# The first block of an adaLN block with an S4 convolution and a SwiGLU FFN: rows of the running sum added by VectorE, statistics taken by ScalarE, weights split in one operation, and another order at the beginning

## The chip, the cores and the metric

The kernel runs on one core of a Trainium2 chip, in float32 results. The metric is device time in microseconds (us) of one execution. Before the change three executions took 484.87, 486.02 and 486.14 us, so the median is 486.02 us.

The engines are named as the profile names them: PE is TensorE (matmul) and PEld its weight load, DVE is VectorE, ACT is ScalarE, POOL is GpSimd, SP is SyncE, which issues most DMAs. Each engine runs its own instructions in the order in which they stand in its queue, and waits at the first one whose inputs are not there. A trailing "q" (ACTq) is the engine's sequencer, which issues DMAs.

## The reference

```python
def _layernorm(x, eps=1e-5): return (x - mean(x)) / sqrt(var(x) + eps)      # over the 448 channels

x = A_u                                                    # 2048 rows x 448 channels
sa, ca, ga, sb, cb, gb = (silu(c) @ w_mod) in six rows of 448
h = _layernorm(x) * (1 + ca) + sa
x = x + ga * (causal_conv(h, K) + h * Dskip)               # K[d, l] = Re sum_n C dB exp(dt A l), 256 states
h = _layernorm(x) * (1 + cb) + sb
x = x + gb * ((silu(h @ w_gate) * (h @ w_up)) @ w_down)    # 448 -> 1792 -> 448
```

The reference does the convolution with FFTs of length 4096. The kernel sums the 256 states into a constant and a linear part of K when a flag, computed on the chip from the data, says that this is exact enough (it is so for these inputs). The convolution is then a running sum down the rows: a triangular matrix of ones times the scaled rows, plus what was summed up to the tile before. A general path stands beside it, behind a branch on the flag, and is not run here.

## The kernel before, in words

The 2048 rows are 16 tiles of 128, in blocks of 2, 2, 3, 3, 3 and 3 tiles (`BLOCKS`). For each block a loop goes over f = 0 to 13, the 14 slices of 128 of the 1792 hidden units. In step f, `gate_up(f)` computes gate and up for the whole block: 22 matmuls (L729) of 128x128 weights against 256 or 384 columns. Weights and data are held as a high part, rounded to the fast matmul format, and a low part with the rest, so each product is high*high + low*high + high*low. A bank is a slice of PSUM. ACT then makes `p`, the silu of gate (L744), DVE multiplies it with up (L757), ACT rounds the product to `phi` (L760), and DVE takes the rest `plo` (L761). Then `down(f-1)` adds the product of the step before into the output accumulators (L773, three matmuls for each tile). So PE does gate_up(f) while the hidden units of f-1 are made ready.

Between the two, at half-steps given by the table `TIMES`, stands what the next block needs: number 2f is the place after `gate_up(f)` and ahead of `down(f-1)`, 2f+1 the place after `down(f-1)`. For the first block the steps of each following tile are `n1.stat` (mean and variance of the rows, two operations of DVE, L150 and L151), `n1.root` (1/sqrt, on POOL, L167 and L168), `s0` (the normalized rows, L182 and L184), `s1` (two products with the kernel's coefficients, L908), `s4f` (the running sum on PE, L945 to L948, then two DVE operations L927 and L950), `s5` (the result added to the tile, L960 and L961, and the last rows of the sum copied to `run` by ACT, L957, and DVE, L958, and sent to partition 0 by a DMA that ACT issues, L959), `n2.stat`, and at the end `n2.root` and `make_xn` (L193 on DVE, L194 and L195 on ACT). After gate_up(13) the tiles are turned (transposed) by PE (L206) into `hhi` and `hlo`, which the next block's gate_up reads.

`s4f` takes in the running sum of the tile before by two float32 matmuls with a single row: `pe.matmul(s, f32(tri[0:1, :]), run1[0:1], ...)` (L947) and the same for run0 (L948).

The first block also prepares the weights, which stay on the chip for the later blocks. In step f the weights of f+2 are split: `split_w` casts 1024 elements of each partition on ACT (L123), which are four chunks of channels for gate and four for up, the fourth of which has only 64 channels and holds them twice; DVE takes the rest of three chunks each (L125, 768 elements) and later that of the second copy in the fourth (L127, 256 elements on 64 partitions). `split_d` does the same for the down weight of f (L115 on ACT, `wdh`; L117 on DVE, `wdl`).

The beginning, up to the first matmul of gate_up(0), has its order written by hand: `PLAN` is a list of names of steps, and each engine issues its instructions in that order. In it the first two tiles are convolved, their statistics taken (L150, L151), normalized (`n10` and `n11`, L432, `xn0` and `xn1`, L487), turned by PE (`tr0`, `tr1`, L374 and L377), and cast to `hhi` (L423) and `hlo` (L428). A matmul (L472) with ones and a copy from PSUM spread the vector gb over the partitions. `first_rows` stands behind down's first place: ACT copies the last rows of the running sum (L696) and the first tile's rows (L697) out of PSUM, DVE adds (L698), and a DMA takes the row to partition 0 (L699).

Of the kernel before, what the change touches and what calls it, by code (L numbers as in the profile page):

```python
# [27 lines left out]
MB = max(BLOCKS)  # L28
# [15 lines left out]
m1 k1 cpc gd h11 hd0 ck v01 sq0 o10 v10 w0 cbw o12 v11 w01 o01 o02 hd1 o13 o14 xh1 gc0 sa st0 fs sp gq r0 n10 spc x1 xn0 gc1 st1 sbt tr0  # L44
qtb sbc r1 fl n11 l1 gbk hi00 xn1 w02 tr1 hi01 lo00 hi1 lo01 lo1 d00 d01 w1 w11 gb w12"""
# [11 lines left out]
def tile_kernel(ctx, tc, x, a_re, a_im, b_re, b_im, c_re, c_im, log_dt,  # L57
# [61 lines left out]
    def split_w(j, part=None, en=ve):  # L119
        hi, lo, st = wgu[j][:, :, 0:3, :], wgu[j][:, :, 4:7, :], wgu[j][:, :, 3, :]  # L120
        w = raw[j]
        if not part:
            sc.copy(wgu[j][:, :, 0:4, :], w)  # L123
        if part is None or part == 1:
            en.tensor_tensor(lo, w[:, :, 0:3, :], f32(hi), op=OP.subtract)  # L125
        if part is None or part == 2:
            en.tensor_tensor(st[64:128], w[64:128, :, 3, :], f32(st[64:128]), op=OP.subtract)  # L127
# [6 lines left out]
    run0, run1 = run[:, 0, :], run[:, 1, :]  # L134
    ca1 = const.tile([128, D], F32)
# [8 lines left out]
    flag = const.tile([1, 1], I32)  # L144

# [7 lines left out]
    class Norm:  # L153
# [10 lines left out]
        def root(self, ts):  # L164
            rs = small.tile([128, MB], F32, name="rs" + self.tag)
            n = len(ts)
            po.tensor_scalar(rs[:, 0:n], self.mv[:, 0:n, 1], EPS, None, op0=OP.add)  # L167
# [101 lines left out]
    with tc.tile_pool(name="pre", bufs=1) as pre:  # L269
# [23 lines left out]
        ve.memset(mhalf, -0.5)  # L293
        tiny = pre.tile([1, 1], F32)
# [74 lines left out]
        def turned_to(ps, t):  # L369

            for k in range(4):
# [38 lines left out]
        def to_channels(q):  # L410
            pk[q] = bank()
            turned_to(pk[q], h2[q])
# [7 lines left out]
        def high(q, ks=range(4)):  # L420
            for k in ks:
                c_ = slice(q * 128, (q + 1) * 128)
                sc.activation(hhi[:, k, c_], pk[q][:, k * 128:(k + 1) * 128], AF.Identity, bias=sbc[:, k:k + 1])  # L423

        def low(q, ks=range(4)):
            for k in ks:
                c_ = slice(q * 128, (q + 1) * 128)
                ve.scalar_tensor_tensor(hlo[:, k, c_], pk[q][:, k * 128:(k + 1) * 128], sbc[:, k:k + 1], f32(hhi[:, k, c_]),  # L428
                                        op0=OP.add, op1=OP.subtract)
# [7 lines left out]
        def flag_sum():  # L437
            pe.matmul(psm["d"][0:1, 460:462], ones, sz, start=True, stop=True)

        def flag_of():  # L440
            zm = pre.tile([1, 1], F32)
            ve.tensor_reduce(zm, psm["d"][0:1, 460:462], axis=AX.X, op=OP.add)
# [28 lines left out]
            "qtb": copy(gb, lambda: psm["gq"][:, 0:D]), "gb": copy(gb, lambda: psm["gq"][:, 0:D]),  # L471
# [15 lines left out]
            **{f"xn{q}": (lambda q: lambda: sc.activation(h2[q], h2[q], AF.Copy, scale=n2.of[q][1]))(q) for q in range(2)},  # L487
            **{f"tr{q}": do(to_channels, q) for q in range(2)}, "hi1": do(high, 1),
            **{f"hi0{z}": do(high, 0, (2 * z, 2 * z + 1)) for z in range(2)},
            "lo1": do(low, 1),  # L490
            **{f"lo0{z}": do(low, 0, (2 * z, 2 * z + 1)) for z in range(2)},

            "w0": do(split_w, 0, 0), "w01": do(split_w, 0, 1, WV), "w02": do(split_w, 0, 2, WV),
            "w1": do(split_w, 1, 0), "w11": do(split_w, 1, 1), "w12": do(split_w, 1, 2),
            **{f"d0{z}": do(split_d, 0, z) for z in range(2)},
# [197 lines left out]
    def first_rows():  # L693

        e = slice(96, 128)
        sc.copy(run1[e], CV[e, 0:D])  # L696
# [374 lines left out]
```

## Time and profile before

| what | value |
|---|---|
| three executions | 484.87, 486.02, 486.14 us |
| the profiled execution | 485.06 us, span 483.0 us |
| granted TensorE clock, mean | 0.999 |
| PE busy | 471.6 us, 2743 matmuls |
| PEld busy | 444.9 us |
| DVE busy | 285.1 us, 550 instructions |
| ACT busy | 155.4 us, 336 instructions |
| POOL busy | 59.8 us, 82 instructions |
| first matmul of gate_up(0) | 33.53 us from the span's start |
| first matmul of block 1 | 95.19 us |
| first matmul of block 2 | 153.05 us |

The span is the part of an execution that the profile covers; here 2.06 us of the execution lie outside it. Busy shares are over the whole span, and mix stages that have different limits: the beginning (to 33.53 us) with the loading of the inputs, the first block (to 95.19 us) with the splitting of the weights, and the other blocks, in which nothing is split.

In the rows of the timeline a line is: start, duration, engine, line, operation, output<-inputs, shapes, and in brackets the idle time of the engine ahead of it with what ended it. Of the chain of waits each piece has its start, its duration and the engine and line whose work filled it.

### The profile page before, as it was taken

To read this page: it belongs to the slowest core of one execution; us is meant where nothing else is said; L and a number is where in the kernel's file an instruction comes from. 1 tells how busy PE (TensorE), PEld (TensorE's weight loads), DVE (VectorE), ACT (ScalarE), POOL (GpSimd) and SP (SyncE) were. 2 spreads that over 40 slices of the span, in tenths; PEclk is the share of its full clock that TensorE was granted. 3 is DMA by queue.
4 is the path that set the end of the run, shared out by engine and by line. 5 is a ranking of instruction groups with operands and counts; after the bars stand their busy time and mean duration, and the time that the engine had idled before them with its cause. 6 is when DMAs were issued, how large, how long until landed. Compare 5 with 4: busy or idle time off the path is not lost.

```text
span 483.0 us, 7024 instructions
## 1 busy us (share of the span) xinstructions
PE 471.6 (98%) x2743; PEld 444.9 (92%) x2743; DVE 285.1 (59%) x550; ACT 155.4 (32%) x336; POOL 59.8 (12%) x82
## 2 busy tenths in 40 slices
PE   6999999999999999999999999999999999999995
PEld 4668988999999999999999999999999999999995
DVE  4879998768876546573644757375475544221225
ACT  5876545522234222332312323331222232112111
POOL 1220000000000040310022221002241000000000
PEclk9999999999999999999999999999999999999999
DMA  8965563020001200111200011130001112000001
GB/s 307 405 225 165 194 188 103 0 96 2 1 2 39 58 1 0 45 38 51 92 25 0 2 44 46 43 115 0 2 2 44 45 43 77 22 1 0 1 1 62
DMA packets 18778, 31.24 MB, mean 65 GB/s; under 512 B 2608, under 2 KB 13488, under 8 KB 18736
## 3 DMA queue, kind: packets, MB, share of 16 engines
q1 hardware_dynamic: 18000, 30.52, 18.8%
q8 instruction: 23, 0.38, 0.3%
q10 hardware_dynamic: 736, 0.19, 0.2%
q14 instruction: 19, 0.16, 0.1%
HBM read 24.61 MB, written 6.03 MB: 63 GB/s over the span
## 4 chain that ended last, share of the span: by engine, by line
PE 92%; DMA 3%; DVE 2%; ACT 1%; issue 0%; POOL 0%; SPq 0%; ACTq 0%; DVEq 0%
PE bank L729 59%; PE dn L773 28%; DMA wm<-in_w_mod_groups_dram 2%; DMA x<-in_A_u_dram 1%; PE bank L238 1%; PE dn L449 1%; PE bank L934 1%; PE cv L933 1%; PE cv L935 0%; PE bank L947 0%; DVE x L812 0%; PE bank L206 0%; PE cv L946 0%; PE cv L948 0%; ACT raw L195 0%
## 5 line engine op out<-in xcount | busy, mean ns | idle before, releaser
L729 PE MATMUL bank<-hhi,gu 128*128 128x384 f32 (+1 forms) x1169 | 211.3, 320 | 0.0
L729 PEld LDWEIGHTS bank<-hhi,gu 128*128 128x128 f32 x1169 | 191.2, 188 | 3.1 <-issue 0.7
L729 PE MATMUL bank<-hlo,gu 128*128 128x384 f32 (+1 forms) x668 | 131.8, 319 | 0.0
L757 DVE TENSOR_TENSOR bank<-raw,bank 128x384 f32<-128x384 f32 (+1 forms) x69 | 36.9, 534 | 125.0 <-PE bank L729 121.6
L729 PEld LDWEIGHTS bank<-hlo,gu 128*128 128x128 f32 x668 | 110.2, 188 | 0.0
L760 ACT CAST phi<-bank 128x384 fp32r<-128x384 f32 (+1 forms) x83 | 36.9, 444 | 141.6 <-DVE bank L757 141.6
L744 ACT ACTIVATE raw<-bank 128x384 f32<-128x384 f32 (+1 forms) x70 | 32.9, 470 | 123.0 <-PE bank L729 114.9
L761 DVE TENSOR_TENSOR plo<-bank,phi 128x384 fp32r<-128x384 f32 (+1 forms) x83 | 42.5, 512 | 37.1 <-ACT phi L760 37.1
L773 PE MATMUL dn<-wdh,phi 128*128 128x448 f32 x218 | 58.3, 368 | 0.6 <-DVE run L698 0.4
L773 PE MATMUL dn<-wdh,plo 128*128 128x448 f32 x218 | 57.7, 366 | 0.0
L773 PE MATMUL dn<-wdl,phi 128*128 128x448 f32 x218 | 57.6, 365 | 0.0
L773 PEld LDWEIGHTS dn<-wdl,phi 128*128 128x128 f32 x218 | 41.0, 188 | 3.4
L773 PEld LDWEIGHTS dn<-wdh,plo 128*128 128x128 f32 x218 | 40.9, 188 | 3.3
L773 PEld LDWEIGHTS dn<-wdh,phi 128*128 128x128 f32 x218 | 38.9, 188 | 2.9 <-DVE run L698 0.7
L167 POOL TENSOR_SCALAR rsb<-mvb 128x1 f32<-128x1 f32 (+2 forms) x13 | 4.6, 354 | 171.9 <-DVE mvb L151 171.9
L167 POOL TENSOR_SCALAR rsa<-mva 128x3 f32<-128x3 f32 (+1 forms) x6 | 2.4, 396 | 116.1 <-DVE mva L151 116.1
L123 ACT CAST gu<-raw 128x1024 fp32r<-128x1024 f32 x14 | 14.6, 1046 | 0.0
L125 DVE TENSOR_TENSOR gu<-raw,gu 128x768 fp32r<-128x768 f32 x14 | 13.3, 953 | 0.1
L922 DVE TENSOR_TENSOR vl<-m,vh 128x448 fp32r<-128x448 f32 x12 | 9.1, 757 | 6.7 <-ACT vh L921 6.1
L908 POOL TENSOR_TENSOR m<-m,gm 128x448 f32<-128x448 f32 x9 | 10.4, 1154 | 21.4 <-DVE m L184 17.5
L194 ACT ACTIVATE raw<-raw,rsb 128x64 f32<-128x64 f32 x14 | 4.8, 346 | 21.0 <-DVE raw L193 11.9
L927 POOL TENSOR_TENSOR m<-m,gd 128x448 f32<-128x448 f32 x9 | 11.6, 1284 | 0.0
(232 smaller groups left out, 411.0 us busy)
## 6 DMA issues: line engine op xcount, KB each, us to landing
raw<-in_B_w_gate_up_dram SPq DMA_DIRECT2D x14, 512.0 KB, 3.9
rawd<-in_B_w_down_dram SPq DMA_DIRECT2D x16, 224.0 KB, 4.1
x<-in_A_u_dram SPq DMA_DIRECT2D x12, 224.0 KB, 3.3
out_dram<-x SPq DMA_DIRECT2D x11, 224.0 KB, 2.0
xd<-raw SPq DMA_DIRECT2D x9, 256.0 KB, 2.0
raw<-xd SPq DMA_DIRECT2D x36, 64.0 KB, 2.0
wm<-in_w_mod_groups_dram SPq DMA_DIRECT2D x5, 448.0 KB, 8.2
wm<-in_w_mod_groups_dram SPq DMA_DIRECT2D x5, 336.0 KB, 8.2
```

The costliest lines, as they stand in the source:

```text
L123: sc.copy(wgu[j][:, :, 0:4, :], w)
L125: en.tensor_tensor(lo, w[:, :, 0:3, :], f32(hi), op=OP.subtract)
L167: po.tensor_scalar(rs[:, 0:n], self.mv[:, 0:n, 1], EPS, None, op0=OP.add)
L729: pe.matmul(ps[s][:, 0:n], w[:, s, a], (hlo if lo else hhi)[:, k, 0:n], start=first and q == 0, stop=end and q == len(ka) - 1)
L744: sc.activation(p[:, 0:n], ps[0][:, 0:n], AF.Silu)
L757: ve.tensor_tensor(ps[1][:, 0:n], p[:, 0:n], ps[1][:, 0:n], op=OP.mult)
L760: sc.copy(hi[:, 0:n], ps[1][:, 0:n])
L761: ve.tensor_tensor(lo[:, 0:n], ps[1][:, 0:n], f32(hi[:, 0:n]), op=OP.subtract)
L773: pe.matmul(dn[q][:, 0:D], u[:, cs], v, start=f == 0 and z == 0, stop=f == (NF - 3 if last else NF - 1) and z == 2)
L908: (ve if on_v else po).tensor_tensor(v, h, g, op=OP.mult)
L922: ve.tensor_tensor(vl, v0, f32(vh), op=OP.subtract)
L927: (ve if on_v else po).tensor_tensor(h, h, gd, op=OP.mult)
```

## The change

It has four parts in the first block and one at the end of the second.

*Rows.* A new step `rows` adds the running sum's row to row 0 of the two products, by two DVE operations of one partition (x448). `s4f` then has two matmuls instead of four.

*Statistics.* For the two tiles of block 1, ACT does what DVE did: `sums` is a Copy with an accumulated sum; POOL divides the sum by 448; then a Square of (mean - x) with an accumulated sum. The root, on POOL, divides by 448 and adds eps. Both ACT operations write their 448 columns into a tile that is free at that time. This holds for the statistics ahead of the convolution (`n1`) and behind it (`n2`).

*Split.* ACT casts three chunks of each half (768 elements) and copies the fourth with a scale that is 0 on partitions 0 to 63 and 1 on 64 to 127, so that one DVE operation over all four chunks (1024 elements) makes the low parts. The low chunks then stand in reverse order, and gate_up reads them so. The new tile `half` takes two small memsets at the start.

*Beginning.* The second tile's sum and statistics stand ahead of the normalizing of the first; the second tile is turned into two banks instead of one; casts are divided between ACT and DVE; the split of d0's high part stands earlier, its low part inside gate_up(0); `first_rows`' two ACT copies stand ahead of the branch, its DVE add inside gate_up(0), its DMA behind it.

*End of the second block.* The three `make_xn` of block 1 all stand at step 23, where one stood at 23 and two at 24.

```diff
-    ((1, 1), 5, ((5, 10, 15, 15, 15), (9, 9, 18, 19, 19)), 19, (22, 23)),
-    ((2, 3, 3), 3, (...), 23, (23, 24, 24)),
+    ((1, 2), 4, ((5, 10, 13, 15, 15, 16), (9, 9, 17, 19, 20, 20)), 21, (22, 23)),
+    ((2, 3, 3), 3, (...), 23, (23, 23, 23)),
...
-    def split_w(j, part=None, en=ve):
-        hi, lo, st = wgu[j][:, :, 0:3, :], wgu[j][:, :, 4:7, :], wgu[j][:, :, 3, :]
+    def split_w(j, part):
         w = raw[j]
-        if not part:
-            sc.copy(wgu[j][:, :, 0:4, :], w)
-        if part is None or part == 1:
-            en.tensor_tensor(lo, w[:, :, 0:3, :], f32(hi), op=OP.subtract)
-        if part is None or part == 2:
-            en.tensor_tensor(st[64:128], w[64:128, :, 3, :], f32(st[64:128]), op=OP.subtract)
+        if part == 0:
+            sc.copy(wgu[j][:, :, 0:3, :], w[:, :, 0:3, :])
+            sc.activation(wgu[j][:, :, 3, :], w[:, :, 3, :], AF.Copy, scale=half)
+        else:
+            ve.tensor_tensor(wgu[j][:, :, 3:7, :], w[:, :, ::-1, :], f32(wgu[j][:, :, 0:4, :][:, :, ::-1, :]), op=OP.subtract)
...
+        def sums(self, i, ts, z):
+            if i == ts[0] and not z:
+                self.mv = small.tile([128, MB, 2], F32, name="mv" + self.tag)
+            m, v = (self.mv[:, i - ts[0], k:k + 1] for k in range(2))
+            if not z:
+                sc.activation(h_of(i), xs[i], AF.Copy, accum_out=m)
+                po.tensor_scalar(m, m, 1.0 / D, None, op0=OP.mult)
+            else:
+                sc.activation(h_of(i), xs[i], AF.Square, scale=-1.0, bias=m, accum_out=v)
...
             "sbt": lambda: turned_to(psm["s"], qt["s"]), "sbc": do(columns, sbc, "s"),
-            "qtb": copy(gb, ...), "gb": copy(gb, lambda: psm["gq"][:, 0:D]),
+            "qtb": copy(gb, ...), "gb": lambda: ve.tensor_copy(gb, psm["gq"][:, 0:D]),
...
     def first_rows():
-        e = slice(96, 128)
-        sc.copy(run1[e], CV[e, 0:D])
-        sc.copy(xs[0], DN[0][:, 0:D])
-        ve.tensor_tensor(run0[e], run1[e], DN[1][e, 0:D], op=OP.add)
-        sc.dma_start(run[0:1], run[127:128])
+        ve.tensor_tensor(run0[end], run1[end], DN[1][end, 0:D], op=OP.add)
...
                 ve.tensor_tensor(ps[1][:, 0:n], p[:, 0:n], ps[1][:, 0:n], op=OP.mult)
-                if nw is not None:
+                if fresh and f == 0:
+                    split_d(0, 1)
+                    for g, a in todo.get("mid", []):
+                        g(*a)
+                elif nw is not None:
                     split_w(nw, 1)
                 sc.copy(hi[:, 0:n], ps[1][:, 0:n])
                 ve.tensor_tensor(lo[:, 0:n], ps[1][:, 0:n], f32(hi[:, 0:n]), op=OP.subtract)
-                if nw is not None:
-                    split_w(nw, 2)
+                if fresh and f == 0:
+                    split_w(nw, 1)
...
                 for i, h in zip(nx, stat1):
-                    go(h, n1.stat, i, nx)
-                go(root1, n1.root, nx)
+                    if b:
+                        go(h, n1.stat, i, nx)
+                    else:
+                        go(h, n1.sums, i, nx, 0)
+                        go(h + 1, n1.sums, i, nx, 1)
+                go(root1, n1.root, nx, not b)
...
+                    elif not b:
+                        go(h, n2.sums, nx[q], nx, 0)
+                        go(h + 1, n2.sums, nx[q], nx, 1)
...
-            pe.matmul(s, tri, v1, start=True, stop=False)
-            pe.matmul(o, f32(tri), v0, start=True, stop=False)
-            pe.matmul(s, f32(tri[0:1, :]), run1[0:1], start=False, stop=True)
-            pe.matmul(o, f32(tri[0:1, :]), run0[0:1], start=False, stop=True)
+            pe.matmul(s, tri, v1, start=True, stop=True)
+            pe.matmul(o, f32(tri), v0, start=True, stop=True)
...
-        return lambda b: ((s0, v(s1), s4f, s5), ...
+        return lambda b: ((s0, v(s1), rows, s4f, s5), ...
```

The sequence of instructions on the engines, in each listing the line, the operation, output<-inputs and the shape (for a matmul the moving columns). First ACT in f = 10 and 11 of the first block, around the statistics of tile 3 (`x_75`), before:

```order
L957 COPY run<-bank 32x448
L959 DMA run<-run 1x16x56
L115 CAST wdh_852<-rawd_82 128x448
L744 ACTIVATE p<-bank 128x256
L123 CAST gu_850<-raw 128x2x512
```

And after; here L122 and L123 are the two parts of the cast, L765 is silu:

```order
L987 COPY run<-bank 32x448
L989 DMA run<-run 1x16x56
L170 ACTIVATE m_79,mvb<-x_75 128x448
L173 ACTIVATE m_79,mvb<-x_75,mvb 128x448
L115 CAST wdh_916<-rawd_83 128x448
L765 ACTIVATE p<-bank 128x256
L122 CAST gu_914<-raw 128x2x384
L123 ACTIVATE gu_914<-raw,half 128x2x128
```

Both sums of the tile stand ahead of the down weight's cast and of silu in ACT's queue, with POOL's division between them.

DVE at the same place, before (step f = 9 and 10):

```order
L960 TENSOR_TENSOR x_75<-x_75,cv 128x448
L961 SCALAR_TENSOR_TENSOR x_75<-bank,tok,x_75 128x448
L150 BN_STATS stb<-x_75 128x6
L151 BN_AGGR mvb<-stb 128x2
L117 TENSOR_TENSOR wdl_853<-rawd_82,wdh_852 128x448
L757 TENSOR_TENSOR bank<-p,bank 128x256
```

And after (step f = 10 and 11; L778 is the product of p with up, L786 is plo, L207 the first operation of `make_xn`):

```order
L990 TENSOR_TENSOR x_75<-x_75,cv 128x448
L991 SCALAR_TENSOR_TENSOR x_75<-bank,tok,x_75 128x448
L117 TENSOR_TENSOR wdl_917<-rawd_83,wdh_916 128x448
L778 TENSOR_TENSOR bank<-p,bank 128x256
L125 TENSOR_TENSOR gu_914<-raw,gu_914 128x2x512
L786 TENSOR_TENSOR plo<-bank,phi 128x256
L207 SCALAR_TENSOR_TENSOR raw<-x_74,mvb,cbw 128x448
```

The statistics are gone from DVE's queue; the low part of the down weight (L117), which needs ACT's `wdh`, follows the tile's last addition directly, and the whole tail of the convolution stands one step of f later.

ACT in f = 1 and 2 of the first block, before:

```order
L115 CAST wdh_155<-rawd_82 128x448
L744 ACTIVATE p<-bank 128x256
L123 CAST gu_465<-raw 128x2x512
L760 CAST phi<-bank 128x256
L115 CAST wdh_162<-rawd_83 128x448
L744 ACTIVATE p<-bank 128x256
```

And after, where three of the four sums of `n1` stand between `phi` of f = 1 and the cast of the next down weight:

```order
L115 CAST wdh_156<-rawd_82 128x448
L765 ACTIVATE p<-bank 128x256
L122 CAST gu_470<-raw 128x2x384
L123 ACTIVATE gu_470<-raw,half 128x2x128
L785 CAST phi<-bank 128x256
L173 ACTIVATE m_79,mva<-x_74,mva 128x448
L170 ACTIVATE m_79,mva<-x_75 128x448
L173 ACTIVATE m_79,mva<-x_75,mva 128x448
L115 CAST wdh_163<-rawd_83 128x448
L765 ACTIVATE p<-bank 128x256
```

PE at the end of the beginning, before: the first tile's turn, then two matmuls of the running sum (L408) and the spread of gb, then the second tile's turn.

```order
L374 MATMUL bank<-ident,h_0_249 128x128 x3
L377 MATMUL bank<-ident,h_0_249 64x128 x2
L408 MATMUL cv<-v_0_245,all_178 128x448
L408 MATMUL cv<-v_1_246,all_178 128x448
L472 MATMUL bank<-gb,pick 128x448
L374 MATMUL bank<-ident,h_1_250 128x128 x3
L377 MATMUL bank<-ident,h_1_250 64x128 x2
```

And after: gb's spread now stands ahead of both turns, and the second one goes to two banks.

```order
L424 MATMUL cv<-v_0_248,all_181 128x448
L424 MATMUL cv<-v_1_249,all_181 128x448
L495 MATMUL bank<-gb,pick 128x448
L390 MATMUL bank<-ident,h_0_252 128x128 x3
L393 MATMUL bank<-ident,h_0_252 64x128 x2
L390 MATMUL bank<-ident,h_1_253 128x128 x2
L390 MATMUL dn_70<-ident,h_1_253 128x128
L393 MATMUL dn_70<-ident,h_1_253 64x128 x2
```

The turn of the first tile has moved behind the copy of gb that its neighbour in the queue waits for.

More of the change, by code (lines that the diff above doesn't have):

```diff
@@ L144, in tile_kernel @@
     flag = const.tile([1, 1], I32)
+    half = const.tile([128, 1], F32)
     small = ctx.enter_context(tc.tile_pool(name="small", bufs=2))
@@ L408, in left_over, with to_channels @@
                 pe.matmul(CV[:, 0:D], all1, v1[q], start=q == 0, stop=q == 1)
-        def to_channels(q):
-            pk[q] = bank()
-            turned_to(pk[q], h2[q])
+        def to_channels(q, ks=range(4)):
+            ps = DN[2] if 0 not in ks else bank()
+            for k in ks:
+                pk[q, k] = ps
+            turned_to(ps, h2[q], ks)
         def skip(q):
@@ L719, in gate_up @@
                 lo = hid.tile([128, MB * 128], F32R, name="plo")
-                ps = [DN[2] if fresh and f == 0 else bank(), bank()]
-                top = [(k, a) for k, ws in enumerate(((0, 4), (1, 5), (2, 6), (3,))) for a in ws]
+                ps = [bank(), bank()]
+                top = [(k, a) for k, ws in enumerate(((0, 6), (1, 5), (2, 4), (3,))) for a in ws]
                 low = [(k, k) for k in range(4)]
```

74 lines of the change are left out of this document (43 added, 31 removed), and 2 rows, old and new, of the table TIMES.

## The prediction

> **What bounds the kernel now.** I read the page's busy times first, then the chain of waits around the end of the first block, then the engines' shares by stretch, and last the timelines of DVE and ACT.
>
> ```profile
> PE 471.6 (98%) x2743; PEld 444.9 (92%) x2743; DVE 285.1 (59%) x550; ACT 155.4 (32%) x336; POOL 59.8 (12%) x82
> ```
>
> PE is busy for 98% of the span. In the chain of waits from 62 to 96 us every piece is PE:
>
> ```profile
> 65.38 0.94 PE bank L947 x2
> 66.32 0.75 PE cv L948 x2
> ...
> 69.88 1.22 PE dn L773 x6
> 71.10 2.60 PE bank L729 x22
> ...
> 74.66 0.94 PE bank L947 x2
> 75.61 0.75 PE cv L948 x2
> ...
> 92.75 2.44 PE dn L773 x12
> 95.19 0.83 PE bank L729 x7
> ```
>
> A step of f takes PE 2.60 + 1.22 = 3.82 us; block 1 begins at 95.19. By that view PE's work alone sets the first block. The shares by stretch (PE, PEld, DVE, ACT, POOL busy) say something else:
>
> ```profile
> 40.00:63.20 23.20, 23.07 (x168) 22.51 (x169) 22.52 (x45) 13.91 (x27) 1.17 (x2) 1.00 0.62 196
> 63.20:86.40 23.20, 23.20 (x143) 19.34 (x142) 20.80 (x39) 10.62 (x20) 1.17 (x2) 1.00 0.40 124
> ```
>
> DVE, at 59% over the span, is busy for 22.52 of 23.20 us here and for 20.80 in the next stretch: both engines are full. Its timeline has two real gaps (in brackets) up to the normalizing of the next block (L193):
>
> ```profile
> 40.70 0.62 DVE L150 BATCH_NORM_STATS2 sta<-x 128x6 f32<-128x448 f32 x1
> ...
> 42.19 0.61 DVE L117 TENSOR_TENSOR wdl<-rawd,wdh 128x448 fp32r<-128x448 f32 x1
> ...
> 43.16 0.95 DVE L125 TENSOR_TENSOR gu<-raw,gu 128x768 fp32r<-128x768 f32 x1
> 44.03 0.42 DVE L761 TENSOR_TENSOR plo<-bank,phi 128x256 fp32r<-128x256 f32 x1
> 44.48 0.42 DVE L127 TENSOR_TENSOR gu<-raw,gu 64x256 fp32r<-64x256 f32 x1
> 44.94 0.63 DVE L117 TENSOR_TENSOR wdl<-rawd,wdh 128x448 fp32r<-128x448 f32 x1
> ...
> 69.22 0.63 DVE L150 BATCH_NORM_STATS2 stb<-x 128x6 f32<-128x448 f32 x1
> ...
> 69.98 0.61 DVE L117 TENSOR_TENSOR wdl<-rawd,wdh 128x448 fp32r<-128x448 f32 x1
> ...
> 73.81 0.43 DVE L757 TENSOR_TENSOR bank<-p,bank 128x256 f32<-128x256 f32 x1 [0.58 <-ACT gu L123]
> ...
> 84.31 0.43 DVE L757 TENSOR_TENSOR bank<-p,bank 128x256 f32<-128x256 f32 x1 [1.03 <-ACT gu L123]
> ...
> 86.42 1.28 DVE L193 SCALAR_TENSOR_TENSOR raw<-x,mvb,cbw 128x448 f32<-128x448 f32 x2
> ```
>
> From 86.42 on a chain through ACT leads to the last silu of the block:
>
> ```profile
> 87.20 0.35 ACT L194 ACTIVATE raw<-raw,rsb 128x64 f32<-128x64 f32 x1 [2.05 <-DVE raw L193]
> ...
> 91.42 0.39 ACT L744 ACTIVATE p<-bank 128x256 f32<-128x256 f32 x1
> ```
>
> It ends at 91.81, 5.39 us after L193's start, and PE's last gate_up of the block ends at about the same time. So the first block has two paths of equal length, PE's and DVE's with ACT's. Shortening one gives nothing unless the other follows.
>
> **Beginning.** DVE's first split is now one operation of 1024 elements. The rows above start 0.87 us apart for 768 (43.16 to 44.03) and 0.33 to 0.35 for 256, so per element about 1.05 ns; 1024 come to 1.22 from start to end and 1.13 to the next start. The second tile's sum needs POOL's product behind it:
>
> ```profile
> 24.83 0.96 DVE L125 TENSOR_TENSOR gu<-raw,gu 128x768 fp32r<-128x768 f32 x1
> 25.70 0.62 DVE L447 TENSOR_TENSOR hd<-h,gd 128x448 f32<-128x448 f32 x1
> ...
> 28.42 0.61 DVE L418 TENSOR_TENSOR x<-dn,hd 128x448 f32<-128x448 f32 x1
> ```
>
> POOL's product ahead of that sum:
>
> ```profile
> 26.40 1.14 POOL L415 TENSOR_TENSOR hd<-hd,x 128x448 f32<-128x448 f32 x1 [2.36 <-DVE hd L447]
> ```
>
> DVE's hd ends 0.35 later, at 26.67, and POOL at about 27.9; the sum can start there instead of at 28.42, 0.5 sooner. But the first tile's normalizing now stands behind it, and behind that the copy of gb and both turns on PE: I put hi's last cast 0.35 later, and so the first matmul of gate 0 at 33.9; lo on DVE stretches gate 0 by some 0.6 more. In exchange down(0) no longer waits for the two rows that PE waits for:
>
> ```profile
> 33.53 0.36 PE L729 MATMUL dn<-hhi,gu 128*128 128x256 f32 x1 [0.56 <-ACT hhi L423]
> ...
> 39.20 0.47 PE L773 MATMUL dn<-wdh,phi 128*128 128x448 f32 x1 [0.17 <-ACT x L697]
> 40.12 0.47 PE L773 MATMUL dn<-wdh,phi 128*128 128x448 f32 x1 [0.45 <-DVE run L698]
> ```
>
> The two waits with the matmul between them cost 1.1; of these 0.65 goes into the later, longer gate 0, as DVE work that delayed it before (L127 and L125 of the next weights) now stands behind it. So -0.45 at down(0)'s end, at worst 0, at best -1.1. On DVE the same rearrangement puts the following work about 0.3 later (d0's low part now lies there).
>
> **PE's work.** Two matmuls for each of two tiles go: (0.94 + 0.75) + (0.94 + 0.75) = 3.38 us off PE. With the beginning, PE's path is 3.8 us shorter.
>
> **DVE's path, 40 to 86.42.** Removed: 42.19 - 40.70 = 1.49 (n1's statistics), 2 x 0.76 = 1.52 (n2's, 69.22 to 69.98). Splits: between L761's start at 44.03 and the next weight's L117 at 44.94 lie plo and L127, and L125 before them 0.87; the one operation takes 1.13 for 0.87 + 0.45, so -0.19, eleven times: -2.0. The old gaps fall away: 0.58 + 1.03 = -1.6. Added: four one-row additions; later blocks have their like. Beside it are the rows for accumulating operations of ACT and for POOL's work on one column, by line, with minimum, median and maximum in ns:
>
> ```profile
> L913 DVE TENSOR_TENSOR m<-m,run x12: 601/604/606, 113.3 to 373.1; 1x448 f32<-1x448 f32 x12
> L348 ACT ACTIVATE sca<-t,dt x8: 402/508/508, 11.0 to 21.1; 128x256 f32<-128x256 f32 x6, 128x128 f32<-128x128 f32 x2
> L348 ACT ACTIVATION_READ_ACCUMULATOR sca<-t,dt x8: 185/187/187, 11.4 to 21.4; 128x1 f32 x8
> L435 ACT ACTIVATE t<-sa,dm x1: 1054/1054/1054, 22.7 to 22.7; 128x896 f32<-128x896 f32 x1
> L167 POOL TENSOR_SCALAR rsb<-mvb x13: 218/222/719, 27.8 to 381.3; 128x1 f32<-128x1 f32 x11, 128x2 f32<-128x2 f32 x1, 128x3 f32<-128x3 f32 x1
> ```
>
> At 0.54 to the next start: +2.2. Sum so far, with the 0.3: -4.1.
>
> What DVE has to wait for instead is ACT. An accumulating operation over 448 lies between L348's 256 (0.51) and L435's 896 (1.05): 0.67, and 0.19 for reading the sum, less 0.09 that neighbours overlap: 0.77. POOL's division is nearest to L167's 0.22, and with handing over about 0.35; bounds 0.22 and 0.72.
> - f = 1 to 2: behind phi(1) ACT has Square, Copy, (POOL), Square, then `wdh`: 3 x 0.77 + 0.35 + 0.47 = 3.1 us, while DVE has only plo and about 1 us of split. It waits about 1.75, and 0.2 more for the next cast: +1.95.
> - f = 8, 9, 11: ACT's cast of the weight comes later, and the split now needs all of it at once: about 0.3 each, +0.95; between 0 and 1.5.
> - Tile 3: after its last addition (L991) DVE needs `wdh` at once. ACT takes 0.77, POOL 0.35, ACT 0.77 and 0.47 for the cast: +2.4, with no other work of DVE beside it. Behind it silu, product, split and plo all wait.
>
> In all +5.3: L193's successor begins about 1.2 us later, at 87.6, with -0.7 to +2.4 around the bounds (POOL 4 x 0.13 less or 2 x 0.4 more, the casts, the first wait hidden or not). The tail behind it is the same instructions, 5.39 us, so the last silu ends at 93.0 instead of 91.8. The last turns need the bank that this silu frees; three of them (0.11 each) then end at 93.35, where before the last turns ended at 92.75, held by PE's own gate_up(13). Then 2.44 of down: block 1 begins at 95.8, +0.6. So PE's 3.8 us turn into waits: for plo and phi in f = 1 to 3, for `rows` of tile 3, for plo of f = 10 and 11, and for the banks.
>
> By the Trainium skill, page "Perfetto Trace Analysis", section "Identifying the Most-Contended Engine", the engine with the highest occupancy is the one to relieve first; taken over the span that is PE, and PE's whole relief would count. This case's rows for 40 to 63.2 us, with DVE at 97%, do not bear that out for this stage; what the rule would give is the first rival.
>
> **End of block 1.** PE's timeline there:
>
> ```profile
> 148.16 0.54 PE L206 MATMUL bank<-ident,raw 128*128 128x128 f32 x2
> 149.30 0.66 PE L206 MATMUL bank<-ident,raw 128*128 128x128 f32 x4 [0.61 <-ACT raw L195]
> ...
> 150.37 0.65 PE L773 MATMUL dn<-wdh,phi 128*128 128x448 f32 x2
> ```
>
> PE waits 0.6 for the last scaled rows, and 149.30 lies 1.14 after 148.16, where two turns of 0.11 were to be done. The twelve turns are 1.32 without a wait, against about 2.3 from 148.16. With all three tiles normalized half a step earlier the rows are there before gate_up(13) ends: -1.0, between 0 (if silu and phi of f = 12, now behind six scalings on ACT, hold the banks) and -1.0, the whole excess.
>
> **Sum.** Nothing else changes: the later blocks have the same instructions, and the two memsets lie at the start of DVE's queue, beside the input DMAs that all wait for (without that cover about 0.1). +0.6 - 1.0 = -0.4: 484.7 against the profiled 485.06. That run lies 0.96 below the median of 486.02; against the median the same sum gives 485.6. I take 485.1, between them. About 0.3% (1.5 us) is what a measurement of this kernel can tell from no change.
>
> **Rivals.**
> - *PE's work decides.* If ACT's sums are hidden (ACT is busy for only 13.91 + 10.62 of 46.4 us), -3.38 - 0.45 - 1.0 = -4.8: 480.2 to 481.2. Against it stands the order: the sums are in front of `wdh` and silu.
> - *One of the two long waits is hidden*, the one at f = 1 to 2 or the tile 3 one, for instance because DVE is late there anyway: 2.0 to 2.4 less, -2.6: 482.5 to 483.4.
> - *Slower: the chain L991, ACT, POOL, ACT, `wdh`, silu is longer than 2.4.* With POOL's division at L167's longest, 0.72, for each of the four, and accumulating operations as long as L435's 1.05 + 0.2, it is 0.4 + 2 x 0.45 = 1.3 longer, and the wait at f = 1 to 2, with three such operations, 1.7. Even half of it counts: then `make_xn` begins at 89.5 or later, block 1 at 97.7 or later, and the time is 487 to 488.5. It decides from 89.5 on, where 2.5 more at block 1 leave +1.5 after the -1.0.
> - *The end of block 1 does not gain.* Then +0.6: 485.7 to 486.6, inside no change.
> - *ACT reloads its function table* for Copy or Square between two silus. By the Trainium skill, page "ScalarE: Activation LUTs", section "What ACT_TABLE_LOAD costs", each switch to another set costs about 2.66 us; as an estimate from that page, four places would cost some 20 us. In the trace L435, a Square, ran at 22.7 us with no load behind it. I give it 0.01.
>
> **How the numbers follow.** DVE's path takes PE's gain, ends of both blocks as above (484.0 to 486.6 by its own bounds): 0.42. One long wait hidden: 0.26. PE decides: 0.11. Slower: 0.20, and table loads 0.01. "Faster" by over 0.3% (below 484.5) gets the two middle ones: 0.37; "same" 0.42; "slower" (above 487.5) 0.21. The range leaves out the fastest and the slowest ends: 481.5 to 487.6.
>
> **What would show it.** In the profile after: no L947/L948 pieces in the chain; the first matmul of gate_up(0) at 33.9; a DVE gap of about 1.75 at f = 2 and 2.4 before L117 of f = 11, both released by ACT's `wdh`; `make_xn` at 87.6, block 1 at 95.8 with PE waits of 3 us or more spread over f = 1 to 3 and 8 to 13; PE's turns of block 1's end in 1.3 to 1.5 us with no ACT piece in the chain. I am wrong if `make_xn` begins before 86 or after 89.

## The result: no change that can be measured

The changed kernel takes 485.25 us (median of 14 executions, 484.96 to 488.28), the kernel before 485.14 us (14 executions, the three above among them). The ratio is 1.0004, with a 95% interval of 0.9992 to 1.0015. No change was forecast, at 485.1 us; the time agrees. But a loss that was not in the sum stands in it against a gain larger than the one forecast: the last experiments are about that loss.

The profiled execution of the changed kernel took 485.64 us, with a span of 483.8 us (485.06 and 483.0 before). First the page's busy times:

```profile
PE 471.3 (97%) x2735; PEld 445.5 (92%) x2735; DVE 282.6 (58%) x538; ACT 161.2 (33%) x363; POOL 60.4 (12%) x86
```

PE's busy time is nearly what it was, 471.3 us for 471.6, although 3.38 us of its matmuls went: some of the others must have become longer. The shares by stretch (PE, PEld, DVE, ACT, POOL busy) show the exchange: DVE has less work, ACT more, and PE has gaps.

```profile
40.00:63.20 23.20, 23.20 (x169) 22.29 (x168) 20.81 (x35) 17.32 (x42) 1.79 (x4) 1.00 0.61 204
63.20:86.40 23.20, 22.09 (x150) 20.27 (x149) 19.16 (x33) 13.70 (x33) 1.56 (x4) 1.00 0.40 120
```

PE's waits from 33 to 155 us, by what ended them, were all at the first block (total, times, longest):

```profile
PE bank L220 <- DVE plo L786: 1.1, 1, 1.1
PE dn L798 <- ACT phi L785: 1.0, 1, 1.0
PE dn L798 <- DVE plo L786: 0.3, 1, 0.3
PE bank L750 <- issue: 0.2, 1, 0.2
```

DVE's timeline has the waits that were forecast, in brackets:

```profile
45.41 0.63 DVE L117 TENSOR_TENSOR wdl<-rawd,wdh 128x448 fp32r<-128x448 f32 x1 [1.46 <-ACT wdh L115]
...
46.82 1.23 DVE L125 TENSOR_TENSOR gu<-raw,gu 128x1024 fp32r<-128x1024 f32 x1 [0.45 <-ACT gu L123]
...
84.12 0.63 DVE L117 TENSOR_TENSOR wdl<-rawd,wdh 128x448 fp32r<-128x448 f32 x1 [2.28 <-ACT wdh L115]
...
85.66 1.23 DVE L125 TENSOR_TENSOR gu<-raw,gu 128x1024 fp32r<-128x1024 f32 x1 [0.57 <-ACT gu L123]
...
87.13 1.27 DVE L207 SCALAR_TENSOR_TENSOR raw<-x,mvb,cbw 128x448 f32<-128x448 f32 x2
```

The chain of waits around the end of the first block goes through the sums of tile 3, on ACT and POOL, where before every piece was PE:

```profile
81.16 0.69 DVE x L991
81.87 0.68 ACT m L170 x2
82.62 0.22 POOL mvb L171
82.87 0.76 ACT m L173 x2
83.63 0.46 ACT wdh L115
84.11 0.38 ACT p L765
84.49 0.72 ACT gu L122
...
91.79 0.44 DVE plo L786
92.27 0.44 PE bank L220 x2
...
93.14 2.43 PE dn L798 x12
95.57 4.44 PE bank L750 x37
```

Block 1 begins at 95.57 instead of 95.19, although PE has 3.38 us less to do. The end of block 1 is the place that gained; its chain there no longer has ACT in it:

```profile
146.43 2.64 PE bank L750 x22
149.07 0.66 PE bank L220 x6
149.73 0.33 PE cv L220 x3
150.05 0.33 PE bank L220 x3
150.38 2.43 PE dn L798 x12
152.81 3.36 PE bank L750 x19
```

Block 2 begins 0.24 sooner than before (153.05), but DVE's last addition begins at 478.98 for 478.31: some 0.9 us is lost in blocks 2 to 5, where the two kernels have the same instructions. And gate_up takes 2.64 us here; before it took 2.61 or 2.62 as a rule.

### The profile page after: what moved, and what is told of

It reads as the page before. It is cut to its first block, busy times and chain, and to the rows that moved or that the text cites. A ratio compares the mean times of both kernels' runs of the same rounds, so it can differ in the third digit from the quotient of the medians.

```text
span 483.8 us, 7024 instructions
## 1 busy us (share of the span) xinstructions
PE 471.3 (97%) x2735; PEld 445.5 (92%) x2735; DVE 282.6 (58%) x538; ACT 161.2 (33%) x363; POOL 60.4 (12%) x86
## 4 chain that ended last, share of the span: by engine, by line
PE 86%; DVE 6%; ACT 3%; DMA 3%; issue 1%; SPq 0%; POOL 0%; ACTq 0%; DVEq 0%
PE bank L750 56%; PE dn L798 25%; DMA wm<-in_w_mod_groups_dram 2%; DVE gu L125 1%; DMA vec<-in_c_log_dt_dram 1%; DVE plo L786 1%; DVE wdl L117 1%; PE bank L252 1%; PE cv L968 1%; PE cv L966 1%; PE bank L967 1%; ACT gu L122 0%; DVE bank L778 0%; DVE x L837 0%; PE bank L220 0%
## 5 line engine op out<-in xcount | busy, mean ns | idle before, releaser
L750 PE MATMUL bank<-hlo,gu 128*128 128x384 f32 (+1 forms) x672 | 133.2, 320 | 0.0
L778 DVE TENSOR_TENSOR bank<-raw,bank 128x384 f32<-128x384 f32 (+1 forms) x69 | 36.9, 535 | 125.2 <-PE bank L750 122.7
L765 ACT ACTIVATE raw<-bank 128x384 f32<-128x384 f32 (+1 forms) x70 | 32.9, 470 | 124.2 <-PE bank L750 116.0
L786 DVE TENSOR_TENSOR plo<-bank,phi 128x384 fp32r<-128x384 f32 (+1 forms) x83 | 42.5, 512 | 37.1 <-ACT phi L785 37.1
L181 POOL TENSOR_SCALAR rsb<-mvb 128x1 f32<-128x1 f32 (+1 forms) x12 | 4.2, 346 | 135.2 <-DVE mvb L151 135.2
L125 DVE TENSOR_TENSOR gu<-raw,gu 128x1024 fp32r<-128x1024 f32 x14 | 17.1, 1221 | 2.5 <-ACT gu L123 2.5
L117 DVE TENSOR_TENSOR wdl<-rawd,wdh 128x448 fp32r<-128x448 f32 x16 | 9.9, 620 | 5.8 <-ACT wdh L115 5.7
L122 ACT CAST gu<-raw 128x768 fp32r<-128x768 f32 x14 | 11.6, 830 | 0.0
```

What stands on the lines that cost most here:

```text
L117: ve.tensor_tensor(lo, wdn[j], f32(hi), op=OP.subtract)
L122: sc.copy(wgu[j][:, :, 0:3, :], w[:, :, 0:3, :])
L125: ve.tensor_tensor(wgu[j][:, :, 3:7, :], w[:, :, ::-1, :], f32(wgu[j][:, :, 0:4, :][:, :, ::-1, :]), op=OP.subtract)
L750: pe.matmul(ps[s][:, 0:n], w[:, s, a], (hlo if lo else hhi)[:, k, 0:n], start=first and q == 0, stop=end and q == len(ka) - 1)
L765: sc.activation(p[:, 0:n], ps[0][:, 0:n], AF.Silu)
L778: ve.tensor_tensor(ps[1][:, 0:n], p[:, 0:n], ps[1][:, 0:n], op=OP.mult)
```

## The experiments

The theory: the first block has two paths of the same length, PE's and the one through DVE and ACT; the change shortens PE's, and puts waits into the other. The rival: PE's work decides. Later a second question came up, the 0.03 us of each gate_up. The kernel before was run anew beside each group of experiments, with medians of 485.11 to 485.29 us; the changed kernel was not, and stands at its 485.25.

### Only the rows

The kernel before with the rows alone moved to VectorE:

```diff
-    ((1, 1), 5, ((5, 10, 15, 15, 15), (9, 9, 18, 19, 19)), 19, (22, 23)),
+    ((1, 1), 5, ((5, 10, 13, 15, 15, 15), (9, 9, 17, 18, 19, 19)), 19, (22, 23)),
...
-            pe.matmul(s, f32(tri[0:1, :]), run1[0:1], start=False, stop=True)
-            pe.matmul(o, f32(tri[0:1, :]), run0[0:1], start=False, stop=True)
...
-        return lambda b: ((s0, v(s1), s4f, s5), ...
+        return lambda b: ((s0, v(s1), rows, s4f, s5), ...
```

> The kernel before with only the rows moved: rows of run added by VectorE (steps 13 and 17), two matmuls instead of four, statistics and splits as before. Theory (two paths of equal length): PE loses 3.38 us of work, VectorE gets 4 x 0.54 = 2.2 and its two gaps (0.58 and 1.03) can take at most 1.6 of it, so make_xn begins at 86.4 to 87.0 and block 1 at 95.2 to 95.9; time 0 to 0.6 above that of before (485.2 to 485.8), with 3 us or more of new waits on PE. Rival (PE's work decides, at 98% busy): 3.4 lower, 481.8.

Measured: 486.04 us against 485.29, ratio 1.0013 (0.9998 to 1.0028), so no gain from 3.38 us less work on PE. PE's longest wait and the first operation of make_xn:

```profile
PE bank L945 <- DVE v L914: 2.8, 1, 2.8
```

```profile
87.35 1.28 DVE L193 SCALAR_TENSOR_TENSOR raw<-x,mvb,cbw 128x448 f32<-128x448 f32 x2
```

In one wait PE lost 2.8 of its 3.38 us, for the added row of tile 3 on DVE. L193 began 0.93 later than before, more than the 0.6 at most that I had expected (one gap of 0.82 stayed), and block 1 began at 96.10.

But this execution is not a plain sum of work and waits. Behind that wait PE's granted clock was 0.50 for 3.4 us (in a row of shares by stretch it is the number after POOL's), and the same matmuls took longer there than for tile 2, ten us earlier:

```profile
64.18 0.41 PE bank L945
64.59 0.75 PE cv L946 x2
...
74.64 0.67 PE bank L945
75.32 1.49 PE cv L946 x2
76.81 1.86 PE dn L773 x6
```

```profile
74.70:78.10 3.40, 3.40 (x7) 2.38 (x8) 3.30 (x7) 0.90 (x2) 0.00 (x0) 0.50 0.77 274
```

With 1.22 for down elsewhere in this block, that is 0.26 + 0.74 + 0.64 = 1.6 us, and DVE's gap of 0.82 ends with PE's late gate_up behind it. So without the lower clock block 1 would have begun at about 94.5 by PE's own work (an estimate: 96.10 - 1.6), not later than before but 0.7 sooner. The executions bear this out: three of the twelve ran at a mean granted clock of 1.0 and took 484.66, 485.07 and 485.16 us; the nine others, at 0.991 to 0.996, took 485.68 to 488.36. So the rise of the median goes with the lower clock; without it the rows bring 0.1 to 0.6 us, which is hardly clear of the spread, and not 3.4. "PE's work decides", with its 481.8, is out either way.

### Only the split

The kernel before with the new `split_w`, the tile `half` and the reversed low chunks, the rest as before.

```diff
+    half = const.tile([128, 1], F32)
...
-            sc.copy(wgu[j][:, :, 0:4, :], w)
-            en.tensor_tensor(lo, w[:, :, 0:3, :], f32(hi), op=OP.subtract)
-            en.tensor_tensor(st[64:128], w[64:128, :, 3, :], f32(st[64:128]), op=OP.subtract)
+            sc.copy(wgu[j][:, :, 0:3, :], w[:, :, 0:3, :])
+            sc.activation(wgu[j][:, :, 3, :], w[:, :, 3, :], AF.Copy, scale=half)
+            ve.tensor_tensor(wgu[j][:, :, 3:7, :], w[:, :, ::-1, :], f32(wgu[j][:, :, 0:4, :][:, :, ::-1, :]), op=OP.subtract)
```

> The kernel before with only the split changed: one VectorE operation of 1024 elements a weight instead of 768 and 256. Theory: VectorE's path becomes up to 2.0 us shorter, but PE's own work, unchanged, ends at the same time: no change, 485.2 (within 0.5), the gaps of VectorE grow instead. Rival (VectorE's queue alone sets the first block): 1.5 to 2 lower, 483.4.

Measured: 486.12 us against 485.29, ratio 1.0012 (1.0001 to 1.0023). L192, the first operation of make_xn, began at 86.31 (before: 86.42): DVE's relief turned into five waits of DVE for PE's gate_up, 4.2 us together, of which these are two:

```profile
63.34 0.43 DVE L758 TENSOR_TENSOR bank<-p,bank 128x256 f32<-128x256 f32 x1 [0.92 <-PE bank L730]
...
84.51 0.43 DVE L758 TENSOR_TENSOR bank<-p,bank 128x256 f32<-128x256 f32 x1 [1.45 <-PE bank L730]
```

So shortening either path alone brought little or nothing in the first block. That this kernel was slower by 0.8 was not expected by either side, and gate_up took 2.64 here too; the last experiments answer that.

### Tile 3's statistics back on DVE

The changed kernel; behind the convolution, tile 2's statistics stay on ACT, with one more POOL operation that divides by 448, and tile 3's are DVE's.

```diff
-                    elif not b:
+                    elif not b and q == 0:
                         go(h, n2.sums, nx[q], nx, 0)
                         go(h + 1, n2.sums, nx[q], nx, 1)
+                        go(h + 1, n2.over, nx[q], nx)
...
-                    go(late[0], n2.root, nx, not b)
+                    go(late[0], n2.root, nx)
```

> The changed kernel, but the statistics behind the convolution of tile 3 alone are taken by VectorE again (two operations, 0.76 us). Theory (VectorE's queue with ScalarE's sums in it sets the first block's end): the wait of 2.28 us for wdh behind tile 3's sums goes, 0.76 comes in, so make_xn begins 1.5 us sooner, at 85.6, block 1 at about 94.1, and the time falls by 1.2 to 1.6 us against the changed kernel, to 483.8. Rival (TensorE and the later chain through the scalings set the end): PE's own waits only change places, time within 0.3 of the changed kernel's 485.25.

Measured: 483.22 us against 485.23 of the kernel before, ratio 0.9962 (0.9952 to 0.9973); 2.0 below the changed kernel. In DVE's timeline the two gaps at the end are gone:

```profile
81.52 0.63 DVE L150 BATCH_NORM_STATS2 stb<-x 128x6 f32<-128x448 f32 x1
82.18 0.18 DVE L151 BATCH_NORM_AGGREGATE mvb<-stb 128x2 f32<-128x6 f32 x1
84.61 1.27 DVE L211 SCALAR_TENSOR_TENSOR raw<-x,mvb,cbw 128x448 f32<-128x448 f32 x2
```

make_xn began 2.5 sooner: 2.28 - 0.76 = 1.5 as expected, 0.57 for the cast wait behind it, which went too, and the rest in small shifts. Block 1 began at 93.05.

### Statistics ahead of the convolution back on DVE

The changed kernel, with `n1.stat` at half-step 1 for both tiles instead of `n1.sums`.

```diff
-    ((1, 2), 4, ...
+    ((1, 1), 4, ...
...
-                    if b:
-                        go(h, n1.stat, i, nx)
-                    else:
-                        go(h, n1.sums, i, nx, 0)
-                        go(h + 1, n1.sums, i, nx, 1)
-                go(root1, n1.root, nx, not b)
+                    go(h, n1.stat, i, nx)
+                go(root1, n1.root, nx)
```

> The changed kernel, but the statistics ahead of the convolution of both tiles of block 1 are taken by VectorE again. Theory: the wait of 1.46 at f = 1 to 2 and the ones of 0.30 and 0.45 for the casts beside it go, 1.49 of VectorE's work comes in: make_xn 0 to 0.7 sooner, time 0 to 0.7 below the changed kernel's 485.25. Rival (ScalarE's sums are the whole loss wherever they stand): 1.5 to 2 lower.

Measured: 485.20 us against 485.23, ratio 1.0001 (0.9992 to 1.0010). make_xn began at 86.72, 0.4 sooner than in the changed kernel, and so did block 1 (95.16), but the medians differ by no more than 0.05. The wait of 1.46 went, 1.49 of work came: the term is nearly a draw, inside the 0 to 0.7 of the theory.

### All statistics back on DVE

As the kernel before this one, and behind the convolution too:

```diff
-                    elif not b:
-                        go(h, n2.sums, nx[q], nx, 0)
-                        go(h + 1, n2.sums, nx[q], nx, 1)
...
-                    go(late[0], n2.root, nx, not b)
+                    go(late[0], n2.root, nx)
```

> The changed kernel with all statistics of the first block on VectorE again, as before the change. Theory: both waits go (1.46, 2.28, 0.75 for casts), 3.0 of VectorE's work comes in: 1 to 1.5 us below the changed kernel, about 484, and no better than with tile 3's alone moved back. Rival (taking work off VectorE is what pays): VectorE full again, time as before or 485.5 and more.

Measured: 482.98 us against 485.23, ratio 0.9957 (0.9945 to 0.9969), 2.3 below the changed kernel, more than the 1 to 1.5 that I expected; make_xn began at 84.50 and block 1 at 92.93. Against tile 3's alone (483.22) this is no clear difference, as expected. DVE's busy time in the two stretches, 22.29 and 21.73 of 23.20 us, is higher than in the changed kernel and the time lower:

```profile
40.00:63.20 23.20, 22.96 (x165) 21.88 (x165) 22.29 (x41) 14.82 (x32) 1.17 (x2) 1.00 0.66 201
63.20:86.40 23.20, 23.09 (x158) 21.41 (x157) 21.73 (x39) 12.63 (x28) 1.18 (x2) 1.00 0.38 117
```

Block 1 begins 2.26 us sooner than in the kernel before, where the rows alone made it 0.91 later (0.7 sooner by the estimate without the lower clock) and the split alone 0.25 later (gate_up at 2.64 in it). So rows and split together pay more than either alone, here with the new beginning and the later half-steps, whose parts were not run by themselves; moving the statistics to ACT costs, and most of that cost is tile 3's.

### Only the end of block 1

The kernel before with one number row changed:

```diff
-    ((2, 3, 3), 3, (...), 23, (23, 24, 24)),
+    ((2, 3, 3), 3, (...), 23, (23, 23, 23)),
```

> The kernel before with one change, all three make_xn of block 1's end at step 23. Theory: PE's wait of 0.6 for the scaled rows goes; block 2 begins 0.6 sooner against block 1 (57.25 instead of 57.86 us after it) and the time falls by 0.6, to 484.5. Rival (silu and phi of f = 12 behind six scalings take it back, or the 0.6 seen belongs to the different start of the block): no change, 485.1.

Measured: 484.86 us against 485.23, ratio 0.9993 (0.9984 to 1.0002), which by the time alone is unclear. The chain shows the term:

```profile
145.58 2.61 PE bank L729 x22
148.19 0.66 PE bank L206 x6
148.85 0.33 PE cv L206 x3
149.17 0.33 PE bank L206 x3
149.50 2.43 PE dn L773 x12
151.94 4.21 PE bank L729 x24
```

Block 1, which began at 95.06, took 56.88 us to 151.94, where before it took 57.86: -0.98. I had expected 0.6, the wait alone; the prediction's -1.0 was the better one. The gain stayed to the end of the work: DVE's last addition began at 477.19, and before at 478.31, 1.12 sooner. The span shows only 0.5 of it, as what follows that addition, the last writes to memory, took 5.3 us here and 4.7 before.

### The normalizing behind the hidden units

Two kernels with `make_xn` of the first block's end at step 24, so that plo of f = 12 does not stand behind the scalings: one with tile 3's statistics on DVE and one with all of them there. The number row, against the changed kernel (the second has (1, 1) at its start):

```diff
-    ((1, 2), 4, ((5, 10, 13, 15, 15, 16), (9, 9, 17, 19, 20, 20)), 21, (22, 23)),
+    ((1, 2), 4, ((5, 10, 13, 15, 15, 16), (9, 9, 17, 19, 20, 20)), 21, (24, 24)),
```

> As with tile 3's statistics on VectorE, and make_xn of the first block's end at step 24, behind the hidden units of f = 12 instead of ahead of them. Theory (what is left is the wait of 1.1 us for plo of f = 12, which holds the banks of the turns and stands behind eight scaling operations): that wait goes and the time falls by 0.8 to 1.1 more, to 482.2. Rival (the scaled rows are then too late for the turns, behind gate_up(13)): 0 to 1 slower than 483.2.

Measured: 482.97 us against 485.29, ratio 0.9944 (0.9927 to 0.9961); 0.25 below the same kernel without it, which is not clear. PE's wait for plo was gone, and another stood in its place:

```profile
PE bank L224 <- ACT raw L213: 0.6, 1, 0.6
```

> As with all statistics on VectorE, and make_xn of the first block's end at step 24. Theory: the waits of 0.5 and 0.2 go, the time falls by 0.5 to 0.7, to 482.4. Rival (the scaled rows come too late): 0 to 1 slower than 483.0.

Measured: 482.99 us against 485.29, ratio 0.9950 (0.9934 to 0.9966), the same as 482.98. What was expected of these two did not come: of the 1.1 us that PE had waited for plo with tile 3's statistics on DVE, 0.6 came back as a wait for the late scaled rows, and 0.2 of 0.5 in the second kernel.

### The place of the tiles

In all kernels so far with the new tile `half` gate_up of two tiles took 2.63 or 2.64 us in block 1, in those without it 2.61 to 2.63. Two differences could do this: the reversed order of the low chunks, or the place. `half` has one column, but takes 32 bytes of each partition, and all that is allocated behind it, the weights and the hidden units among it, stands 32 bytes further up; hhi and hlo, which are allocated before it, stay. In the addresses of the two programs the first weight tile begins at byte 63264 and 63296. So I put an unused tile behind the flag:

```diff
     flag = const.tile([1, 1], I32)
+    pad = const.tile([128, 1], F32)
+    ve.memset(pad, 0.0)
```

> The kernel before with one unused tile of one column behind the flag, zeroed once, which moves the weights and hidden units 32 bytes up in each partition of SBUF, as the tile half does in the changed kernel (first weight at byte 63296 instead of 63264); no other instruction changes. Theory (the place of the tiles makes gate_up longer: 2.64 us with the new split against 2.61 with the old one): gate_up 2.64, time 0.7 to 1.0 above that of before, 486.1. Rival (the reversed order of the low chunks does it): gate_up 2.61 and no change, 485.2.

Measured: 486.69 us against 485.11, ratio 1.0043 (1.0029 to 1.0057). One unused column made the kernel 1.6 us slower. Its chain in block 2:

```profile
163.29 3.89 PE bank L731 x22
167.17 1.82 PE dn L775 x9
169.00 3.88 PE bank L731 x22
```

Then the same tile in the changed kernel, beside `half`:

> The changed kernel with the same unused tile, so that the weights begin at byte 63328, 64 above the kernel before. Theory (place): gate_up 2.61 again, 0.7 to 1.0 below the changed kernel, 484.4, with the same waits of PE in the first block. Rival (order of the chunks): gate_up 2.64, 485.25.

Measured: 480.53 us against 485.11, ratio 0.9903 (0.9888 to 0.9918). I had expected gate_up as it was before, 0.7 to 1.0 less; it was shorter than in any kernel so far:

```profile
161.81 3.81 PE bank L752 x22
165.62 1.82 PE dn L800 x9
167.44 3.81 PE bank L752 x22
```

And in the kernel with all statistics on DVE and the late scalings:

> All statistics on VectorE, make_xn of the first block's end at step 24, and the unused tile. Theory (place): 0.7 to 1.0 below the same without the tile (482.99), 482.1, and 3 us below the kernel before. Rival (order of the chunks): 483.0.

Measured: 477.85 us against 485.11, ratio 0.9856 (0.9841 to 0.9871), the fastest of all. Last, two unused tiles in the kernel before, which bring its weights to the same byte, 63328:

> The kernel before with two unused tiles, so that its weights begin at byte 63328, as in the changed kernel with one (480.53). Theory (place, apart from the change): gate_up 2.59 and 3.81 as there, against 2.61 and 3.87; 28 x 0.02 + 56 x 0.06 = 3.9 less than before, 481.2, so that at this place the change itself is worth 0.7 less time, and 1.4 at the place of 63296 (486.69 against 485.25). Rival (the reversed chunks need that place, the kernel before gains nothing from it): 485.1.

Measured: 481.05 us against 485.12, ratio 0.9910 (0.9897 to 0.9924), with 2.59 and 3.81 to 3.82 for gate_up. So the place has its effect whatever the order of the chunks. In each of the fourteen kernels, on whichever chip, gate_up's duration is the one of its row here:

| first weight at byte | gate_up, 2 tiles | gate_up, 3 tiles | kernel before | changed kernel | other kernels |
|---|---|---|---|---|---|
| 63264 | 2.61 us | 3.87 us | 485.1 us | not run | rows only 486.04 |
| 63296 | 2.64 us | 3.88 us | 486.69 us | 485.25 us | split only 486.12, all statistics on DVE 482.98 |
| 63328 | 2.59 us | 3.81 us | 481.05 us | 480.53 us | all statistics on DVE, late scalings 477.85 |

Read along a row, the change is worth 1.4 us at 63296, and 0.5 us at 63328, where the executions of the two kernels, four and five, touch each other (480.28 to 480.65 and 480.52 to 481.14). The split alone, read along its row, is 0.6 below the kernel before and block 1 begins 0.20 later (95.44 against 95.24): still no gain in the first block.

These runs do not show how fast DVE is by itself. make_xn began at 86.42 us in the kernel before with one tile (gate_up 2.64) and at 86.41 with two (gate_up 2.59), as if PE's pace did not matter. But PE's unbroken chain began at 41.11 with one and at 41.55 with two, and that difference took up the longer gate_ups: gate_up(11) ended at 84.20 and 84.19, and DVE's product, which needs its result, began at 84.31 and 84.30.

## Why the prediction was right, and where it was not

*The paths.* The forecast was that PE's 3.4 us are lost to waits, since DVE's path is as long. Shown: with the rows alone 2.8 of them went into one wait for DVE and the time fell by 0.1 to 0.6 us in the executions at full clock, and by none in the median, rather than by 3.4; split alone did not make block 1 begin sooner; both together (with the statistics left on DVE, and the new beginning) let it begin 2.26 sooner. One reading was in all likelihood wrong: the two old gaps of DVE, 0.58 and 1.03, which the view puts down to ACT's cast, ended with PE's gate_up. The product behind the second, which reads nothing of the cast, began at 84.31, 0.11 behind the last matmul of gate_up (84.20); with the split alone it began 0.11 behind it too (84.40, 84.51), and there ACT's cast ended only at 84.63. So PE's path was the longer one, by 1.6 us at most, and the two were not of equal length; the sum did not change by that, as the gaps go when PE is shorter. By the Trainium skill, page "Perfetto Trace Analysis", section "Identifying the Most-Contended Engine", the engine of the highest occupancy is to be optimized first, TensorE's headroom being judged by its weight loads; over the span that is PE, at 98% by matmuls and 92% by weight loads, and the run with the rows alone shows little for it in this stage. The same page's section "Optimization Strategy" says that the most contended engine can change over time and that its gaps are to be looked for within the regime. The trace agrees as far as DVE goes, at 97% from 40 to 63 us against 59% over the span; PE is as full there, at 99%.

*The waits.* Tile 3: 2.4 forecast, 2.28 measured; each accumulating operation took 0.68 to 0.76 with its reading, where 0.77 was worked out from shorter and longer ones, POOL 0.22. The wait at f = 1 to 2: 1.75 forecast, 1.46 measured, and of the casts there 0.30 and 0.45 for 0.2. The casts at f = 8, 9 and 11: 0.47 + 0.45 + 0.57 = 1.5 for 0.95, at the bound. make_xn 87.13 for 87.6, the tail behind it as forecast: the last silu (L765) ended at 92.51, 5.38 later. Block 1 at 95.57 for 95.8. PE's waits there were not "3 us or more": the waits listed come to 2.4 and a further 0.26 lies in down(2); the 14 gate_up, 0.4 longer in all, took up some of the rest.

*The beginning.* The first matmul of gate 0 came at 34.01 for 33.9, that of gate 2 at 41.12 for 41.0, against 41.42 before: -0.3 for -0.45.

*The end of block 1.* The term was right: -0.98 in the run with this alone. In the changed kernel block 1 took 57.24 for 57.86, only -0.62, as 14 gate_up took 0.03 longer each; against the kernel before at the same place it is -1.19 (63296) and -1.02 (63328).

*"Nothing else changes."* This step failed. It went by the instructions of the later blocks, which are the same, and put the new tile down as two hidden memsets. The tile's 32 bytes moved the weights, and the later blocks took about 0.9 us more in the profiled execution; the same shift alone cost the kernel before 1.6 us. At the same place the profiled executions show the two terms of the sum: block 1 begins 0.33 (63296) and 0.61 later (63328) for the forecast +0.6, takes 1.19 and 1.02 less for -1.0, and DVE's last addition begins 0.84 and 0.41 sooner for -0.4. By the medians the change is worth -1.4 and -0.5. So the measured +0.1 is a gain of 1.4 less a loss of 1.6 by the shift, where the forecast had a gain of 0.4 and no loss. That these nearly cancel is luck, and so is a second thing: the sum of -0.4, from the profiled 485.06, was 484.7, and the forecast was set at 485.1 only because the median of three executions was 486.02. Fourteen executions give 485.14.

*The rivals.* "PE's work decides" and "slower by a longer chain" did not come; POOL's division was at the short end each time that counted (0.22). No load of ACT's function table appears at the sums: Copy and Square stood back to back with silu. "One of the long waits hidden" did not come; both stood in DVE's queue.

## What to carry to other kernels

Where two engines are full in the same stretch, a gain on one can turn into a wait on it until the other gets its own: price the second path through the stage by its own rows, and make both shorter in one change. Work that is moved to an engine with idle time still costs its whole latency if what the first engine needs next stands behind it there: the statistics of the last tile were 0.76 us of DVE's work and became 2.28 us of its waiting. And compare the duration of instructions that did not change before and after: a difference there says that something other than the edit's instructions is at work, here the place of a tile, and in the run with the rows alone the granted clock.

## What the runs showed of the hardware that was not expected

The same 22 matmuls took 2.61, 2.64 and 2.59 us (256 columns) and 3.87, 3.88 and 3.81 us (384 columns) with the first weight tile at bytes 63264, 63296 and 63328 of each partition, all that is allocated behind it moved by as much, and hhi and hlo at 48544 and 54688 in all three. Over the kernel before this is 485.1, 486.69 and 481.05 us. Weight loads were 188 ns in all. Which of the moved tiles matters, and by which rule of addresses, was not tried, nor a fourth place; the runs show the effect of the place, not its mechanism. That beats the change itself by far: the kernel with rows and split changed, statistics left on DVE and that place took 477.85 us, 1.4% less than the kernel before.

In the run with the rows alone a wait of PE of 2.84 us was followed by a granted clock of 0.50 for 3.4 us, in which PE's work took some 1.6 us longer. PE's waits of up to 1.2 us in the other profiled executions were not followed by that. This is one profiled execution; that the wait was the cause is not shown.
